# Another order of all pieces in a chunked attention with a gated convolution: the third weight unit behind the second block's keys and queries

## The chip, the cores and the metric

The kernel runs on one core of one Trainium2 chip. The metric is the device time of one execution in microseconds. Engines are named as in the profile: PE (TensorE: matmuls; PEld is its loading of weights), DVE (VectorE), ACT (ScalarE), POOL (GpSimd), and SP (SyncE), which issues all transfers between memory and the chip. PSUM is where matmuls leave their results, here in four banks of two halves each.

## What is computed

Attention runs inside chunks of 64 tokens, for 8 sequences of 576 tokens and 8 heads of 64; its output x is gated by a causal convolution over five tokens and goes through two 512 by 512 matrices, all in float32.

```python
scores = scale * np.matmul(q_c, k_c.transpose(0, 1, 2, 4, 3))      # q_c, k_c, v_c: chunks of 64 tokens
scores = scores - np.max(scores, axis=-1, keepdims=True)
attn = np.exp(scores)
attn = attn / (np.sum(attn, axis=-1, keepdims=True) + 1e-09)
out = np.matmul(attn, v_c)
...
for k in range(K):                                                  # K = 5 taps, per channel
    gate_pre += conv_w[k][None, None, :] * xp[:, k:k + S, :]
gate = 1.0 / (1.0 + np.exp(-gate_pre))
val = x @ w_val
return (gate * val @ w_out).astype(np.float32)
```

## The kernel before

The 4608 tokens are nine groups g of 512, the 512 channels two pairs p of two heads' couples. The work is cut into small functions, called pieces, and one long text, ORDER (lines 19 to 84), lists all 1034 pieces with their arguments. The last loop of the kernel walks through the list and records each piece's instructions, and every engine runs its own share in that order. So ORDER is the whole schedule: on each engine an instruction waits for those that stand before it, and for the data that it needs. SLOTS (lines 87 to 98) says which buffer each piece takes that asks for one (z for buffers of 4 KB a partition, b for PSUM banks, e for the two buffers of exponentials); a buffer that is given out again makes its new writer wait for its old readers.

The pieces that the text speaks of, with g the group, p the pair, c a unit of weights:

- loads on SP: lq, lk, lv (queries, keys, values of g and p; for group 0 the first two also in halves of 256 KB), lw (a unit of w_val "v" or w_out "o", 512 KB), lc (the taps); st and s1 store results.
- weights: each 64-bit number is cut into a high and a low part of fewer bits, so that three cheap products give a float32 product. w1 to w8 make the high part (v_hi, o_hi) on DVE, ACT and POOL, wa and wb the low part (v_lo, o_lo); for units v 1 to v 3 the low part is summed on PE by Q and cast by wc on ACT.
- attention: S multiplies queries by keys (32 small matmuls per g and p, each of which PE runs as two), mx and ng take and scale the maximum on DVE; either sb, ex and sm (subtract, exponential, sum), or ea (16 small exponentials on ACT that sum as they go, 8 for a half) and rc or ra and rr; nm scales on POOL or DVE; T transposes on PE, ec copies to the chip's memory on ACT; A multiplies by the values. xr, xc, xd take its result as high part, as itself and as low part.
- gate: k0 is the first tap on ACT (k0D on DVE), k the other four on DVE (kx and kk do two groups at once), sg the sigmoid on ACT.
- products: V makes one third of the value product (one matmul of 512 columns for group 0, else three), vc copies it on ACT, gs multiplies by the gate on DVE, gr and gd cut the result into high and low part (gd on POOL, gdD on DVE), P is the output product (three matmuls), oc copies it (ocD on DVE). Group 8 ends in smaller pieces, o1 and s1.
- W runs idle matmuls on a zeroed tile before the first data are there: so many of 512 columns, so many of 64.

Every instruction carries line 139 in the profile, since one helper records it; tiles tell them apart: b is a PSUM bank, z and ys are buffers, e_row the exponentials, warm the idle tile.

```python
for piece in ORDER.split(","):
    name, *args = piece.split()
    args = [int(a) if a.isdigit() else a for a in args]
    if name in on_vector:
        fn, on = on_vector[name]
        fn(*args, **{"copy" if fn in (w6, ec, xc, oc, o1, wc) else "on": on})
    else:
        pieces[name](*args)
```

Of the kernel before, what the change touches and what calls it, by code (L numbers as in the profile page):

```python
# [18 lines left out]
ORDER = """zw,lw v 1,zr 1,zr 0,lc,zi,zs 0,zs 1,lw v 3,lw v 2,w1 v 1,w5 c 0,w1 c 0,w2 v 1,w3 v 1,w5 v 1,w4 v 1,w2 c 0,w3 c 0,w5 v 3,  # L19
w7 v 1,w1 v 3,w6 v 1,w8D v 1,w2 v 3,w4 c 0,w3 v 3,W 9 22,Q v 1,lk 0 1 0,lq 0 1 0,w1 v 2,w4 v 3,w2 v 2,w3 v 2,w5 v 2,w6D v 3,  # L20
S 0 1 0,lk 0 0 0,lk 0 1 1,lq 0 1 1,lq 0 0 0,lk 0 0 1,lq 0 0 1,w4 v 2,wc v 1,mx 0 1 0,w6 v 2,w7 c 0,ng 0 1 0,w7 v 2,ea 0 1 0,ra 0 1 0,
W 3,S 0 1 1,w8D v 2,S 0 0 0,mx 0 1 1,w8D c 0,w9,ng 0 1 1,w7 v 3,S 0 0 1,lw v 0,lk 1 0,lq 1 0,lv 0 1,lw o 3,ea 0 1 1,ra 0 1 1,
rr 0 1 0,Q v 2,w8 v 3,mx 0 0,nm 0 1 0,sb 0 0,Q v 3,w5 v 0,w1 v 0,ex 0 0,T 0 1 0,w3 v 0,rr 0 1 1,S 1 0 0,wc v 2,sm 0 0,
nm 0 1 1,S 1 0 1,ec 0 1 0,w2 v 0,A 0 1 0,lk 1 1,lq 1 1,lv 0 0,lv 1 0,wc v 3,mx 1 0,T 0 1 1,nm 0 0,xr 0 1 0,ec 0 1 1,
V 0 2 2 0,sb 1 0,V 0 3 2 1,w5 o 3,A 0 1 1,xc 0 1 0,xr 0 1 1,w4 v 0,T 0 0,xc 0 1 1,xd 0 1 0,V 0 2 3 0,w6D v 0,V 0 3 3 0,
ec 0 0,V 0 2 3 1,w1 o 3,S 1 1 0,w7 v 0,ex 1 0,xd 0 1 1,A 0 0,w8 v 0,k0 0 2,sm 1 0,S 1 1 1,wa v 0,xc 0 0,V 0 0 2 0,V 0 2 2 1,
V 0 0 3 1,V 0 0 2 1,xr 0 0,mx 1 1,V 0 1 2 0,nm 1 0,V 0 0 3 2,V 0 3 3 1,k0 0 0,V 0 3 2 2,V 0 2 3 2,xd 0 0,V 0 3 1 0,
V 0 1 2 1,V 0 0 0 0,V 0 3 3 2,V 0 3 0 0,lw o 0,lw o 2,lw o 1,w5 o 0,k0 0 3,ng 1 1,k 0 0 1,T 1 0,k0 0 1,wbD v 0,V 0 0 0 2,
w2 o 3,V 0 3 2 0,k 0 0 2,V 0 2 1 1,ec 1 0,V 0 2 0 0,V 0 0 1 0,k 0 3 1,V 0 1 0 0,V 0 2 0 1,ea 1 1,V 0 2 0 2,w3 o 3,V 0 2 1 2,
k 0 1 1,V 0 3 1 1,V 0 0 2 2,V 0 1 1 1,w4 o 3,V 0 3 0 1,V 0 2 2 2,V 0 3 1 2,w1 o 1,A 1 0,k 0 0 3,w7 o 3,w1 o 0,V 0 1 3 2,  # L30
# [636 lines left out]
```

## Time and profile before

| | us |
|---|---|
| median of 3 runs | 280.74 (280.64 to 281.19) |
| profiled execution | 281.55 |
| its span, first to last instruction | 279.6 |
| PE busy | 268.9 (96%) |
| DVE busy | 239.5 (86%) |
| ACT busy | 198.7 (71%) |
| POOL busy | 59.4 (21%) |

The profiled execution is a run of its own, 0.8 us above the median; what lies outside the span (some 2 us) is start and end of the program. Times within the trace count from the span's start. Busy shares are averages; what sets the end is read from the chain that ended last, which goes back from the last instruction, at each step to what released it. A piece of that chain called "issue" is time in which an engine waited for nothing that the profile shows.

### The profile page before, as it was taken

Reading aid. Unit: us, or ns where it says so; the run is one execution under the profiler, and the core shown is the slowest. Engines: PE = TensorE matmul, PEld = TensorE weight load, DVE = VectorE, ACT = ScalarE, POOL = GpSimd, SP = SyncE. Lnnn points to the kernel's source line nnn. Section 1 sums busy time; section 2 is a strip of 40 time slices with the busy share of each in tenths; the row PEclk is TensorE's granted clock in tenths of the full one; section 3 lists DMA queues with packets and bytes.
Section 4 is the critical chain, followed back from the end, with each engine's and each line's share of the span. In section 5 each row is a group of like instructions: output and inputs, shape, how many; then the busy total and the mean of one; then the engine's idle time right before and its main releaser. Section 6 shows DMA issues by size and latency. Waiting matters only on the chain.

```text
span 279.6 us, 7851 instructions
## 1 busy us (share of the span) xinstructions
PE 268.9 (96%) x3370; PEld 216.6 (77%) x3370; DVE 239.5 (86%) x303; ACT 198.7 (71%) x368; POOL 59.4 (21%) x58
## 2 busy tenths in 40 slices
PE   6598999999998999999999999999999999999995
PEld 3366778887886888888888888888888888888884
DVE  3979999999999988989898998999999998996020
ACT  5899999999997988895958588837644544614402
POOL 1056242049294003061335001100000000300000
PEclk9999999999999999999999999999999999999999
DMA  6999999763831649540082000000000000050656
GB/s 224 395 409 406 406 407 409 290 225 108 281 149 37 192 150 338 189 131 30 2 292 88 2 5 2 0 0 2 0 0 0 4 0 0 16 212 0 241 209 225
DMA packets 14754, 42.46 MB, mean 152 GB/s; under 512 B 1536, under 2 KB 1792, under 8 KB 14720
## 3 DMA queue, kind: packets, MB, share of 16 engines
q1 hardware_dynamic: 14720, 41.97, 40.7%
q8 instruction: 26, 0.43, 0.6%
q14 instruction: 8, 0.07, 0.1%
HBM read 32.53 MB, written 9.44 MB: 150 GB/s over the span
## 4 chain that ended last, share of the span: by engine, by line
PE 89%; DMA 8%; issue 1%; SPq 0%; ACT 0%
PE b L139 89%; DMA z<-in_v 4%; DMA z<-in_moe_w_val 2%; DMA z<-in_q 2%; SPq L139 0%; ACT z L139 0%
## 5 line engine op out<-in xcount | busy, mean ns | idle before, releaser
L139 PE MATMUL b<-z,v_hi 128*128 128x512 f32 x288 | 97.3, 403 | 1.3 <-issue 1.1
L139 PE MATMUL b<-o_hi,z 128*128 128x512 f32 (+1 forms) x296 | 94.5, 391 | 0.0
L139 DVE SCALAR_TENSOR_TENSOR ys<-ys,cw 128x511 f32<-128x511 f32 (+7 forms) x104 | 84.5, 863 | 0.1
L139 ACT COPY z<-b 128x1024 f32<-128x1024 f32 (+2 forms) x53 | 50.3, 970 | 38.3 <-PE b L139 35.5
L139 PEld LDWEIGHTS b<-z,v_hi 128*128 128x128 f32 x288 | 53.8, 188 | 14.5 <-issue 1.7
L139 PEld LDWEIGHTS b<-o_hi,z 128*128 128x128 f32 x296 | 55.1, 188 | 12.6
L139 PE MATMUL b<-o_lo,z 128*128 128x512 f32 (+1 forms) x148 | 57.4, 388 | 0.0
L139 PE MATMUL b<-z,v_lo 128*128 128x512 f32 x144 | 55.9, 394 | 0.0
L139 POOL TENSOR_TENSOR z<-e_row,rs 128x1024 f32<-128x1024 f32 (+1 forms) x15 | 27.0, 1804 | 47.2 <-DVE rs L139 17.0
L139 PEld LDWEIGHTS b<-o_lo,z 128*128 128x128 f32 x148 | 27.8, 188 | 5.9
L139 PEld LDWEIGHTS b<-z,v_lo 128*128 128x128 f32 x144 | 27.1, 188 | 5.4
L139 POOL TENSOR_TENSOR z<-ys,z 128x1024 fp32r<-128x1024 f32 x4 | 10.0, 2527 | 96.9 <-ACT z L139 96.9
L139 ACT ACTIVATE ys<-ys 128x1024 f32<-128x1024 f32 x16 | 16.8, 1059 | 11.0 <-DVE ys L139 10.8
L139 ACT ACTIVATE e_row<-b,mx 128x64 f32<-128x64 f32 x80 | 23.7, 345 | 0.4 <-DVE mx L139 0.4
L139 DVE TENSOR_TENSOR z<-b,z 128x1024 fp32r<-128x1024 f32 (+1 forms) x19 | 22.0, 1161 | 2.3 <-ACT z L139 1.3
L139 ACT CAST z<-ys 128x1024 fp32r<-128x1024 f32 x16 | 16.5, 1048 | 9.0 <-DVE ys L139 9.0
L139 DVE TENSOR_REDUCE mx<-b 128x16 f32<-128x1024 f32 (+1 forms) x19 | 21.6, 1144 | 1.3 <-PE b L139 1.1
L139 PEld LDWEIGHTS b<-z,z 64*64 64x64 f32 x960 | 15.7, 135 | 7.8 <-DMA z<-in_k 2.6
L139 PE MATMUL b<-z,z 64*64 64x64 f32 x960 | 17.6, 221 | 3.7 <-DMA z<-in_q 3.0
L139 ACT CAST z<-b 128x1024 fp32r<-128x1024 f32 (+1 forms) x19 | 18.7, 991 | 2.1 <-PE b L139 2.1
L139 ACT ACTIVATE ys<-ys,cw 128x512 f32<-128x512 f32 (+1 forms) x25 | 19.2, 811 | 0.0
L139 ACT ACTIVATION_READ_ACCUMULATOR e_row<-b,mx 128x1 f32 x80 | 19.0, 238 | 0.0
(74 smaller groups left out, 308.3 us busy)
## 6 DMA issues: line engine op xcount, KB each, us to landing
out<-z SPq DMA_DIRECT2D x16, 512.0 KB, 3.7
z<-in_q SPq DMA_DIRECT2D x10, 512.0 KB, 7.2
z<-in_v SPq DMA_DIRECT2D x9, 512.0 KB, 5.0
ys<-in_v SPq DMA_DIRECT2D x9, 512.0 KB, 10.1
ys<-in_k SPq DMA_DIRECT2D x9, 512.0 KB, 7.3
z<-in_k SPq DMA_DIRECT2D x7, 512.0 KB, 9.4
ys<-in_q SPq DMA_DIRECT2D x6, 512.0 KB, 10.2
z<-in_moe_w_val SPq DMA_DIRECT2D x4, 512.0 KB, 5.4
```

Source lines behind the costliest of these rows:

```text
L139: return tc.keep_in_program_order(fn(*args, **kwargs))
```

## The change

ORDER and SLOTS are replaced; no function changes. Both lists hold 1034 pieces. Apart from their places, these differ: W 16 16 and W 2 for W 9 22 and W 3; w2 of unit v 2 on DVE instead of w6 of v 3; the first tap of groups 6 and 7 for one couple on ACT (kx 6 1) and that of group 8's last couple on DVE (k0D 8 3); some copies of groups 3, 4 and 6, the scaling of groups 5 and 6 and the gd of group 3 change engines one for one; o1 8 3 goes from DVE to ACT; both gd of group 8 go from DVE to POOL. All else is order. The first and the last line of ORDER and one of SLOTS:

```diff
-ORDER = """zw,lw v 1,zr 1,zr 0,lc,zi,zs 0,zs 1,lw v 3,lw v 2,w1 v 1,w5 c 0,w1 c 0,w2 v 1,w3 v 1,w5 v 1,w4 v 1,w2 c 0,w3 c 0,w5 v 3,
...
+ORDER = """zw,lw v 1,zr 1,zi,zs 0,zs 1,lc,lw v 3,lk 0 1 0,zr 0,lq 0 1 0,w1 v 1,w3 c 0,w2 v 1,w3 v 1,w1 c 0,w2 c 0,w4 v 1,w5 v 3,w1 v 3,
...
-    e="0 1 0 0 0 0 1 1 0 0 0 1 0 1 1 0 1 0",
...
+    e="0 1 0 0 0 0 1 1 0 1 1 0 1 0 1 0 1 1",
```

SP's first transfers, before (in_moe_w_val: a unit of w_val; in_k and in_q: halves of group 0's keys and queries):

```order
L139 DMA z_76<-in_moe_w_val 128x1024
L139 DMA raw_cw<-in_moe_conv_w 128x40
L139 DMA z_90<-in_moe_w_val 128x1024
L139 DMA z_92<-in_moe_w_val 128x1024
L139 DMA z_152<-in_k 128x512
L139 DMA z_154<-in_q 128x512
L139 DMA z_181<-in_k 128x512
```

and now:

```order
L139 DMA z_76<-in_moe_w_val 128x1024
L139 DMA raw_cw<-in_moe_conv_w 128x40
L139 DMA z_89<-in_moe_w_val 128x1024
L139 DMA z_91<-in_k 128x512
L139 DMA z_94<-in_q 128x512
L139 DMA z_166<-in_moe_w_val 128x1024
L139 DMA z_91<-in_k 128x512
```

The third unit of weights moved behind the first halves of keys and queries.

ACT around the two first groups of exponentials (e_row<-b,mx, eight each), before; the casts write v_hi from a buffer and v_lo from a PSUM bank:

```order
L139 CAST v_lo<-b_148 128x2x256
L139 CAST v_hi<-z_156 128x2x256
L139 ACTIVATE e_row_65,rs_197<-b_164,mx_191 128x64 x8
L139 ACTIVATE rs_197<-rs_197,e_row_65 128x8
L139 ACTIVATE e_row_65,rs_278<-b_211,mx_246 128x64 x8
L139 ACTIVATE rs_278<-rs_278,e_row_65 128x8
L139 ACTIVATE z_303<-z_268 128x512
```

and now:

```order
L139 ACTIVATE z_186<-z_166 128x512
L139 ACTIVATE e_row_65,rs_193<-b_149,mx_184 128x64 x8
L139 ACTIVATE rs_193<-rs_193,e_row_65 128x8
L139 CAST v_hi<-z_188 128x2x256
L139 CAST v_lo<-b_174 128x2x256
L139 ACTIVATE e_row_65,rs_275<-b_204,mx_231 128x64 x8
L139 ACTIVATE rs_275<-rs_275,e_row_65 128x8
L139 ACTIVATE z_300<-z_221 128x512
```

A cast to v_hi and the cast to v_lo moved from ahead of the first group to between the two.

PE from the transposes of group 0, pair 0 (T, ident with 128x128) to its values (A, x32) and the scores of group 1, pair 1 (S, x16 each), before:

```order
L139 MATMUL b_419<-ident,z_388 128x128 x8
L139 MATMUL b_393<-z_390,v_hi 128x512 x2
L139 MATMUL b_393<-z_390,v_lo 128x512
L139 MATMUL b_439<-z_373,z_375 64x64 x16
L139 MATMUL b_459<-z_434,z_377 64x64 x32
L139 MATMUL b_439<-z_373,z_375 64x64 x16
L139 MATMUL b_515<-z_390,v_hi 128x512
```

and now:

```order
L139 MATMUL b_417<-ident,z_383 128x128 x8
L139 MATMUL b_407<-z_386,v_hi 128x512
L139 MATMUL b_407<-z_386,v_lo 128x512 x2
L139 MATMUL b_407<-z_386,v_hi 128x512
L139 MATMUL b_407<-z_386,v_lo 128x512
L139 MATMUL b_443<-z_432,z_361 64x64 x32
L139 MATMUL b_480<-z_411,z_359 64x64 x32
L139 MATMUL b_519<-z_386,v_hi 128x512
```

Five products of 512 columns stand between transposes and values instead of three, and both halves of the scores follow the values. SP loads these values one place earlier than before, and the keys of group 1, pair 1 behind them.

## Rows read from the trace of the kernel before

**Rows 1.** The page: busy us of each engine with its share of the span and its instructions; from its list of DMA queues the one that brings instructions (packets, MB, share).

```profile
PE 268.9 (96%) x3370; PEld 216.6 (77%) x3370; DVE 239.5 (86%) x303; ACT 198.7 (71%) x368; POOL 59.4 (21%) x58
...
q8 instruction: 26, 0.43, 0.6%
```

**Rows 2.** The chain of work that ended last, in order of time: start, us, what.

```profile
2.10 6.26 DMA z<-in_moe_w_val
...
8.38 5.37 DMA z<-in_q
...
13.77 11.88 DMA z<-in_v
...
25.78 5.95 PE b L139 x118
31.73 0.17 issue
31.90 52.88 PE b L139 x1014
84.78 0.90 issue
85.68 191.00 PE b L139 x1883
```

**Rows 3.** Stretches of 10 us: their mean, then the busy time (and instructions) of PE, PEld, DVE, ACT and POOL, the granted clock of TensorE, the busy share of the DMA engines, and GB/s.

```profile
20.00:30.00 10.00, 9.05 (x220) 7.16 (x209) 9.01 (x14) 9.30 (x16) 6.37 (x4) 1.00 1.03 406
...
50.00:60.00 10.00, 10.00 (x197) 8.36 (x199) 9.78 (x17) 9.97 (x31) 3.17 (x2) 1.00 0.63 241
...
80.00:90.00 10.00, 9.10 (x163) 7.29 (x162) 9.27 (x13) 8.81 (x11) 6.55 (x6) 1.00 0.01 5
```

**Rows 4.** SP's issues in order of time, the thirteenth and the fourteenth: start, duration, what.

```profile
9.03 0.33 SPq L139 DMA_DIRECT2D z<-in_moe_w_val  x1
9.70 0.33 SPq L139 DMA_DIRECT2D z<-in_k  x1
```

**Rows 5.** PE in order of time, with the idle time before a row and what ended it.

```profile
1.19 4.16 PE L139 MATMUL b<-warm 128*128 128x512 bf16 x31 [1.19 <-DVE warm L139]
...
9.82 0.69 PE L139 MATMUL b<-z,z 64*64 64x64 f32 x32 [1.39 <-DMA z<-in_q]
...
18.32 1.16 PE L139 MATMUL b<-z,z 64*64 64x64 f32 x64 [0.43 <-DMA z<-in_q]
...
24.66 0.69 PE L139 MATMUL b<-z,z 64*64 64x64 f32 x32
25.78 1.63 PE L139 MATMUL b<-z,z 64*64 64x64 f32 x96 [0.43 <-DMA z<-in_v]
27.34 0.50 PE L139 MATMUL b<-z,v_hi 128*128 128x512 f32 x1
...
30.69 1.04 PE L139 MATMUL b<-ident,z 128*128 128x128 f32 x8
```

**Rows 6.** ACT in order of time.

```profile
6.44 0.70 ACT L139 ACTIVATE z<-z 128x512 fp32r<-128x512 uint32 x1 [0.33 <-DMA z<-in_moe_w_val]
...
10.08 0.56 ACT L139 CAST v_lo<-b 128x512 fp32r<-128x512 f32 x1
10.82 0.62 ACT L139 CAST v_hi<-z 128x512 fp32r<-128x512 f32 x1 [0.18 <-DVE z L139]
11.69 0.31 ACT L139 ACTIVATE e_row<-b,mx 128x64 f32<-128x64 f32 x1 [0.25 <-DVE mx L139]
...
14.40 0.29 ACT L139 ACTIVATE e_row<-b,mx 128x64 f32<-128x64 f32 x1
...
17.09 0.68 ACT L139 ACTIVATE z<-z 128x512 f32<-128x512 uint32 x1
...
24.05 1.01 ACT L139 COPY z<-b 128x1024 f32<-128x1024 f32 x1 [0.32 <-issue]
...
25.91 0.71 ACT L139 ACTIVATE ys<-ys,cw 128x512 f32<-128x512 f32 x1
```

**Rows 7.** PE in order of time, from 81.7 to 85.7 us.

```profile
81.70 0.40 PE L139 MATMUL b<-o_hi,z 128*128 128x512 f32 x1
82.03 1.16 PE L139 MATMUL b<-ys 64*64 64x64 f32 x64
83.01 1.11 PE L139 MATMUL b<-z,ys 64*64 64x64 f32 x64
84.06 0.50 PE L139 MATMUL b<-z,v_hi 128*128 128x512 f32 x1
84.39 0.39 PE L139 MATMUL b<-z,v_lo 128*128 128x512 f32 x1
85.68 0.50 PE L139 MATMUL b<-z,v_hi 128*128 128x512 f32 x1 [0.90 <-issue]
```

**Rows 8.** Groups of like instructions (all of the trace): how often, busy us and mean ns of one, then idle time before them.

```profile
L139 DVE TENSOR_SCALAR z<-z 128x512 uint32<-128x512 uint32 x16 | 6.7, 417 | 0.0
...
L139 DVE SCALAR_TENSOR_TENSOR z<-z 128x512 uint32<-128x512 uint32 x8 | 5.5, 685 | 0.3 <-ACT z L139 0.3
...
L139 DVE TENSOR_SCALAR mx<-mx 128x8 f32<-128x8 f32 x2 | 0.3, 168 | 0.0
...
L139 DVE COPY z<-b 128x1024 f32<-128x1024 f32 x3 | 3.7, 1220 | 12.2 <-PE b L139 12.2
...
L139 DVE TENSOR_SCALAR ys<-ys,cw 128x1024 f32<-128x1024 f32 x1 | 0.7, 746 | 0.0
...
L139 DVE TENSOR_SCALAR z<-tails,cw 128x512 f32<-128x512 f32 x1 | 0.5, 479 | 0.0
...
L139 DVE TENSOR_TENSOR z<-z,z 128x1024 fp32r<-128x1024 f32 x2 | 2.4, 1222 | 1.1 <-ACT z L139 1.1
...
L139 ACT ACTIVATE z<-z 128x1024 f32<-128x1024 f32 x2 | 2.0, 1054 | 5.6 <-DVE z L139 5.6
...
L139 POOL TENSOR_TENSOR z<-ys,z 128x1024 fp32r<-128x1024 f32 x4 | 10.0, 2527 | 96.9 <-ACT z L139 96.9
```

**Rows 9.** PE in the output products of the last group: three matmuls each.

```profile
267.17 0.63 PE L139 MATMUL b<-o_hi,z 128*128 128x512 f32 x2
...
267.87 0.63 PE L139 MATMUL b<-o_hi,z 128*128 128x512 f32 x2
```

More of the change, by code (lines that the diff above doesn't have):

```diff
@@ new lines @@
+w7 v 1,w2 v 3,w3 v 3,w5 v 1,w4 v 3,w6 v 1,w8D v 1,W 16 16,S 0 1 0,lw v 2,lk 0 1 1,lq 0 1 1,w5 c 0,w6 v 3,w7 v 3,Q v 1,
+lq 0 0 0,lk 0 0 0,lk 0 0 1,lq 0 0 1,mx 0 1 0,w5 v 2,w1 v 2,w4 c 0,ng 0 1 0,w3 v 2,ea 0 1 0,ra 0 1 0,w2D v 2,S 0 1 1,lw v 0,
+lq 1 0,lk 1 0,lv 0 1,w7 c 0,w4 v 2,mx 0 1 1,W 2,S 0 0 0,w7 v 2,ng 0 1 1,w6 v 2,rr 0 1 0,wc v 1,w8D v 2,S 0 0 1,ea 0 1 1,
+ra 0 1 1,nm 0 1 0,Q v 2,mx 0 0,w8 v 3,sb 0 0,T 0 1 0,w5 v 0,Q v 3,lw o 3,w1 v 0,ex 0 0,rr 0 1 1,w8D c 0,w3 v 0,wc v 2,
+S 1 0 0,nm 0 1 1,sm 0 0,w2 v 0,S 1 0 1,ec 0 1 0,T 0 1 1,lq 1 1,lv 0 0,wc v 3,mx 1 0,A 0 1 0,nm 0 0,ec 0 1 1,xr 0 1 0,
@@ new lines @@
+A 0 1 1,sb 1 0,xc 0 1 0,V 0 2 2 0,xr 0 1 1,V 0 3 2 0,lk 1 1,V 0 3 2 1,xc 0 1 1,w1 o 3,T 0 0,w9,w4 v 0,k0 0 2,V 0 3 3 0,
+w3 o 3,V 0 2 3 1,ec 0 0,w7 v 0,V 0 2 2 1,V 0 2 3 0,w6D v 0,V 0 3 3 1,w8 v 0,xd 0 1 0,ex 1 0,A 0 0,xd 0 1 1,w5 o 3,hc 0 1,
+S 1 1 0,sm 1 0,wa v 0,xr 0 0,S 1 1 1,V 0 0 2 0,xc 0 0,V 0 1 2 1,mx 1 1,V 0 1 1 0,nm 1 0,V 0 2 1 0,V 0 1 0 0,w2 o 3,
+V 0 3 0 0,V 0 0 0 0,xd 0 0,k0 0 3,V 0 3 1 0,V 0 0 3 2,V 0 3 0 1,k0 0 0,V 0 2 1 1,V 0 1 3 0,k 0 3 1,T 1 0,wbD v 0,V 0 0 2 2,
+V 0 3 1 2,ng 1 1,k 0 0 1,V 0 0 1 0,lw o 1,lv 1 0,V 0 2 1 2,V 0 3 2 2,k 0 3 2,V 0 2 2 2,V 0 3 1 1,V 0 3 0 2,V 0 0 1 1,
@@ new lines @@
+sb 8 1,k0 5 0,V 4 2 3,k0 4 1,V 5 0 0,hc 5 1,kk 4 2 2,hc 4 0,ex 8 1,hc 4 1,T 7 1,k0 5 1,kk 4 2 3,V 4 2 1,ec 7 1,V 5 0 3,
+k 5 1 1,vc 4 1,A 7 0,sm 8 1,A 6 1,xr 7 0,nmD 8 1,T 8 0,xc 7 0,V 5 1 1,kk 4 2 4,ec 8 0,V 5 0 1,xc 6 1,k 5 0 1,V 5 1 0,xd 7 0,
+V 5 0 2,xr 6 1,V 5 2 0,kk 4 3 2,V 5 1 3,T 8 1,xd 6 1,V 5 3 3,ec 8 1,k 4 0 3,V 5 1 2,kk 4 3 3,A 6 0,vc 5 0,k 4 1 1,A 8 0,
+xr 6 0,A 8 1,xr 8 0,xcD 6 0,V 5 3 1,xc 8 0,xd 6 0,hc 6 0,V 5 2 1,kx 6 0,V 5 2 2,xd 8 0,xr 8 1,V 5 3 2,k 5 0 2,V 6 2 0,
+k 4 0 4,V 5 2 3,kk 4 3 4,V 8 0 0,V 6 3 3,k 5 1 2,sg 5 1,V 5 3 0,xd 8 1,V 6 3 0,vc 5 1,V 6 2 2,kk 6 0 1,sg 4 1,V 8 1 2,
@@ new lines @@
+V 7 3 0,gs 5 0,V 7 2 1,V 7 1 2,gdD 4 0,V 7 2 3,vc 7 0,V 8 3 0,k 3 3 2,vc 6 0,V 8 2 3,kk 6 1 4,k0 8 0,P 4 0 0,kk 6 3 3,
+gr 5 0,P 4 1 2,P 4 0 1,sg 7 0,k 3 3 3,V 8 3 3,kk 6 2 2,vc 7 1,P 4 1 1,sg 6 0,P 4 2 0,kk 6 3 4,V 8 2 1,gdD 5 0,P 4 2 1,
+P 4 0 2,gdD 5 1,V 8 3 1,P 4 2 3,kk 6 2 3,P 4 3 0,gs 6 0,V 8 2 2,P 4 3 2,vc 8 1,gs 7 0,P 5 0 0,gr 6 0,P 4 0 3,k 3 2 3,
+P 5 2 0,kk 6 2 4,P 5 0 3,k 3 1 2,sg 6 1,P 5 2 1,k 3 2 4,P 4 1 0,k 3 0 2,P 5 0 1,gs 6 1,P 4 1 3,P 5 0 2,gdD 6 0,oc 4 0,
+P 4 2 2,sg 7 1,k 3 3 4,P 4 3 1,k0D 8 2,gr 7 0,P 5 2 3,k 8 2 1,P 4 3 3,gs 7 1,P 6 2 0,oc 4 1,P 5 1 1,gr 6 1,st 4 1,P 6 0 0,
@@ new lines @@
+P 3 1 3,gs 8 0,P 3 3 2,P 3 1 2,gs 8 1,gr 8 0,P 3 0 1,gr 8 1,P 6 2 1,P 6 2 3,oc 7 1,gd 8 1,P 3 2 2,ocD 6 1,st 7 1,P 3 1 0,
+P 3 0 2,st 6 1,P 3 1 1,gd 8 0,P 3 0 3,P 3 3 1,ocD 3 0,P 3 3 3,P 3 2 1,st 3 0,st 7 0,P 3 2 3,st 5 1,P 8 3 0,st 6 0,P 8 2 0,
+P 3 3 0,P 8 0 0 0,oc 3 1,P 8 3 2,P 8 3 3,st 3 1,st 5 0,P 8 0 1 0,P 8 0 3 0,st 4 0,P 8 2 3,P 8 3 1,P 8 1 0,P 8 1 2,P 8 2 2,
+P 8 2 1,P 8 1 3,o1 8 2,o1 8 3,P 8 1 1,s1 8 2,s1 8 3,P 8 0 0 1,o1 8 1,P 8 0 2 0,P 8 0 3 1,s1 8 1,o1 8 0 0,P 8 0 1 1,s1 8 0 0,
+P 8 0 2 1,o1 8 0 1,s1 8 0 1"""
```

111 lines of the change are left out of this document (43 added, 68 removed), and 12 rows, old and new, of the table z.

## The prediction

> **What bounds the kernel now.** I read the page's busy times first: TensorE is busy for 96% of the span, VectorE for 86% [rows 1]. The chain that ended last then says where the other 4% lie: three landings of loads up to 25.64 us, and from 25.78 to 276.68 us nothing but matmuls, with two short pieces called "issue", 0.17 us at 31.73 and 0.90 us at 84.78 [rows 2]. So the end is fixed by the time at which TensorE comes to run without gaps, by the matmul work that is left then, and by these two holes. VectorE, ScalarE and GpSimd count only where they make TensorE wait. The reader is to see that there are about 30 us in which an order can gain, and that elsewhere it can only lose.
>
> What the two holes are can be told from counts. TensorE runs 3370 matmuls and 3370 weight loads, and the instruction queue q8 brings 26 packets, 259 instructions each [rows 1]. Between the two holes lie 1014 matmuls [rows 2], with their loads 2028 instructions, or 7.8 packets; with the semaphore instructions that no row counts, about eight. I take both for waits for the next packet of TensorE's own code. Before the second hole, two runs of 64 small matmuls and two large ones, 260 instructions, pass in 2.75 us (82.03 to 84.78), and work goes on 3.65 us after they began [rows 7]; the DMA engines are nearly idle there (share 0.01) [rows 3]. Before the first hole the last 128 matmuls begin about 25.2 us, and work goes on 6.7 us later, at a DMA share of 1.03 [rows 2, 3, 5]. TensorE stood until 25.78 us for a load inside that stretch, so perhaps only 6.1 us of it belong to the code.
>
> **The change, part by part.** The profiled execution took 281.55 us at a span of 279.6, the median of the runs shown is 280.74; I work out differences on the trace and add them to the median. The reordering adds or removes no matmul except idle ones that keep the array running (34 as before).
>
> *Loads.* From the ninth on, SP issues a transfer when the eighth before it has landed; the chain shows it for the twelfth, which follows the landing of the third weight unit at 8.36 us, and by the next two issues the first keys and queries landed about 9.0 and 9.7 us [rows 2, 4]. At 406 GB/s [rows 3] 512 KB take 1.29 us. With keys and queries ahead of the third weight unit, the first scores can start about 8.4 us instead of 9.82 [rows 5]; the unit lands about 9.7, and behind it each place in the queue keeps its time. The longer idle run (16 wide matmuls) ends about 8.9 us if each takes 0.43 us as the first ones do (nine and 22 short ones end at 5.35 [rows 5]); if it does, up to 0.5 us of the 1.4 are lost.
>
> *VectorE and ScalarE up to the second exponentials.* The first maximum waits now for VectorE: behind the landing of the second weight unit (6.4 us [rows 6]) stand four instructions of 0.42 and two of 0.69 us, 3.1 us, so it starts about 9.4, ends at 10.1, and with one word split and two short ones (0.42 and 0.17 each) [rows 8] the first exponentials start at 10.6 to 11.0 instead of 11.69 [rows 6]. They take 2.7 us to the next group (11.69 to 14.40). But the order puts the cast of the third unit and the v_lo eviction, 0.62 and 0.56 us long, between the two groups of exponentials, where they stood ahead of both [rows 6]. So the second group starts at 14.3 to 14.9, against 14.40. I take no change: **the early scores are spent on ScalarE before they reach TensorE.**
>
> *TensorE from 18 to 32 us.* Keys and queries of the second group keep their place, so the score run at 18.32 stays. ScalarE's list from 17.09 to the copy at 24.05 has the same pieces; one weight scaling moves out, one tap of about 0.7 us moves in [rows 6]. That copy feeds the run that waited at 25.78 for values landing at 25.64; these are now one place earlier in the queue, 24.4 [rows 2]. So this run starts when the copy ends, 24.7 to 25.1 us, 0.7 to 1.1 earlier. Ahead of it the order has eight large matmuls instead of five, behind it the two score runs together (96 records took 1.56 us, so 128 take 2.1), and then the cast of its result, which is free only behind the copy, the exponential and a weight scaling, about 27.1 to 27.6. Twelve matmuls at 0.233 later the transposes start at 30.0 to 30.5 instead of 30.69, with one large matmul more done: 0.4 to 0.9 us gained by the data. [...] I take 31.45 and the one matmul: **-0.55 us** (from -0.9 to +0.3).
>
> *The middle.* A change between small and large matmuls costs about 0.1 us: from 81.70 the step to the small run is 0.33 us, and from 84.06 that to the second large matmul is 0.33 too, where 0.23 is usual [rows 7]. From here the orders have 61 and 58 such changes, some of them free: **+0.1**. Scores of group 5 and the values product behind them stand together as before, so the hole of 0.90 stays. The dense stretch near 55 to 60 us meets one load more in the queue; where before the DMA share falls to 0.63 [rows 3], a packet of code can come late there: 0 to 0.9 us, I take **+0.15**. Up to its last tap VectorE has one tap (0.75 us) and one eviction (1.22, which stands behind that tap now) less and one tap (0.48) more [rows 8]; it does not bound TensorE, whose chain has no VectorE piece [rows 2].
>
> *The end.* Group 8's last two subtractions go from VectorE (1.22 us each) to GpSimd (2.53 each) [rows 8]. From the last tap to the end of both it takes a sigmoid (1.05, the first of the two runs beside the last tap), two gate products (2.4), a cast (1.05) and 5.1 us on GpSimd, about 9.6 us, with the hand-overs 10.3. In the order 17 output pieces of 0.70 us (three matmuls, 267.17 to 267.87 [rows 9]) cover that, 11.9 us, where 13 stood: nothing, unless the last tap comes over 1.6 us later than its place. The last copy and store are the same.
>
> Sum: -0.55 + 0.1 + 0.15 = -0.3, so **280.4 us**.
>
> **Rivals.** *Code is no limit (faster).* If the transposes are held by data alone and the hole at 31.73 is gone, the start gives 0.9; if the one at 84.78 shrinks as well, another 0.9. Against it: two idle times without a releaser, eight packets apart. This gives 279.0 to 279.9. [...]
>
> *Code is late in the loaded stretch (slower).* The place is the dense run of scores and values near 57 us, where more loads are outstanding: 260 instructions pass in about 4.5 us, and if the packet needs 6.1 us as at 31.9, TensorE stands 1.0 to 1.5 us. It decides from a wait over about 5 us. With the start anywhere from the forecast's -0.55 to 0 this gives 281.2 to 282.2.
>
> *The early load does not come early (slower, and the change not doing what it says).* Transfers share the engines; if the first queries land less than about 0.6 us earlier, the two pieces between the exponentials cost ScalarE 0.5 us and more, and everything behind follows: +0.2 to +0.8, 281.0 to 281.5.
>
> **How the numbers follow.** Forecast (280.0 to 281.0) 0.52; no limit by code (279.0 to 279.9) 0.25; late code (281.2 to 282.2) 0.13; no early load 0.10. The range from 279.3 to 281.6 leaves out about a fifth. About 0.2% (0.56 us) is what a measurement of this kernel can tell from no change. Faster than 280.18 holds the second case and a quarter of the first, 0.38; slower than 281.30 holds most of the late code and part of the last, 0.15; the rest, 0.47, is within.
>
> **What would show it.** The first scores at about 8.4 to 8.9 us; the second group of exponentials near 14.4; the values run at 24.7 to 25.1; an "issue" hole right behind the transposes near 31 us and one of about 0.9 near 84 us; no other wait of TensorE over 0.3 us. I am wrong if the second group of exponentials starts before 13.8, if the hole near 31 us is missing, if a new one stands between 50 and 65 us, or if TensorE waits for GpSimd after 255 us.

## Result and profile after the change

The changed kernel is slower: 282.29 us (median of 20 runs, 280.44 to 284.32) against 280.72 (20 runs, 279.68 to 282.26), a ratio of 1.0053 with a 95% interval of 1.0032 to 1.0074, or 1.5 us. The profiled execution took 283.19 us at a span of 281.1, 1.6 us above that of the kernel before (281.55); they lie 0.9 and 0.8 us above their medians.

The chain of waits of the changed kernel (start, us, what) answers to [rows 2]:

```profile
1.65 6.08 DMA z<-in_moe_w_val
...
21.52 0.64 PE b L139 x4
...
23.52 8.85 PE b L139 x163
32.38 0.25 issue
32.63 52.83 PE b L139 x1014
85.46 0.65 issue
86.11 33.20 PE b L139 x268
...
119.33 1.02 ACT z L139
...
120.37 4.83 DMA out<-z
...
125.55 1.02 ACT z L139
...
126.60 1.24 DVE z L139
...
127.88 150.22 PE b L139 x1402
```

As many matmuls are left at 32.63 us as at 31.90 before, and at 86.11 as at 85.68. So the start loses 0.73 us; between the two holes nothing is lost (52.83 against 52.88); the second hole is 0.25 shorter; and from it to the end TensorE takes 191.99 us instead of 191.00, of which 0.54 is idle time in a wait that the kernel before did not have. Together 1.42 us, the whole difference of the last matmul's end (278.10 against 276.68). Among PE's idle times by releaser, 0.5 us behind VectorE's z are new.

The start, in the timeline of PE, DVE and ACT (start, duration, what, idle time before it and what ended it); it answers to [rows 5, 6]:

```profile
9.19 0.69 PE L139 MATMUL b<-z,z 64*64 64x64 f32 x32 [1.03 <-DMA z<-in_q]
16.30 0.79 PE L139 MATMUL b<-v_hi,signed 128*128 128x512 f32 x1
26.52 0.69 PE L139 MATMUL b<-z,z 64*64 64x64 f32 x32
7.75 1.10 DVE L139 TENSOR_SCALAR z<-z 128x512 f32<-128x512 f32 x3 [1.82 <-DMA z<-in_moe_w_val]
10.53 0.68 DVE L139 TENSOR_REDUCE mx<-b 128x8 f32<-128x512 f32 x1
11.81 0.32 ACT L139 ACTIVATE e_row<-b,mx 128x64 f32<-128x64 f32 x1 [0.60 <-DVE mx L139]
14.60 0.60 ACT L139 CAST v_hi<-z 128x512 fp32r<-128x512 f32 x1
15.11 0.58 ACT L139 CAST v_lo<-b 128x512 fp32r<-128x512 f32 x1
15.58 0.32 ACT L139 ACTIVATE e_row<-b,mx 128x64 f32<-128x64 f32 x1
```

The second weight unit lands at 7.7 us (VectorE takes it up at 7.75 after 1.82 us of idling) instead of 6.3, and the first queries, which stand behind it in the queue, at 9.05 (TensorE takes them up at 9.19). So the first maximum is hardly earlier than before, and the two ScalarE pieces between the groups of exponentials put the second group at 15.58 instead of 14.40 [rows 6].

The new wait, in the timeline of ACT, DVE and PE:

```profile
125.55 1.01 ACT L139 CAST z<-b 128x1024 fp32r<-128x1024 f32 x1 [1.38 <-DMA out<-z]
126.60 1.23 DVE L139 TENSOR_TENSOR z<-b,z 128x1024 fp32r<-128x1024 f32 x1 [1.03 <-ACT z L139]
127.88 1.09 PE L139 MATMUL b<-ident,z 128*128 128x128 f32 x8 [0.54 <-DVE z L139]
```

A copy (xr 4 1) is written into the buffer from which output block (1, 0) is being stored. The store was issued at 120.37 and took 4.83 us behind the transfers in flight (DMA share 0.97, 0.92 and 0.98 from 120 to 126 us, in steps of 2); the copy waits for it, the difference behind the copy (xd 4 1) waits too, and the transposes T 5 1 wait for the PSUM bank that both read. This comes from the table of buffers (SLOTS), which was replaced with the order.

### The profile page after: what moved, and what is told of

Same layout as the page of the kernel before. It is cut to its first block, busy times and chain, and to the rows that moved or that the text cites. A ratio compares the mean times of both kernels' runs of the same rounds, so it can differ in the third digit from the quotient of the medians.

```text
span 281.1 us, 7859 instructions
## 1 busy us (share of the span) xinstructions
PE 271.6 (97%) x3370; PEld 217.1 (77%) x3370; DVE 236.5 (84%) x300; ACT 199.6 (71%) x369; POOL 67.3 (24%) x60
## 4 chain that ended last, share of the span: by engine, by line
PE 88%; ACT 5%; DMA 4%; DVE 1%; issue 1%; SPq 0%; ACTq 0%
PE b L139 88%; DMA z<-in_moe_w_val 2%; ACT z L139 2%; ACT e_row L139 2%; DMA out<-z 2%; DVE z L139 1%; ACT v_lo L139 0%; SPq L139 0%; DVE mx L139 0%; ACT v_hi L139 0%; ACT rs L139 0%; ACTq L139 0%; DVE cw_h L139 0%
## 5 line engine op out<-in xcount | busy, mean ns | idle before, releaser
L139 DVE SCALAR_TENSOR_TENSOR ys<-ys,cw 128x509 f32<-128x509 f32 (+7 forms) x104 | 84.6, 864 | 0.1
L139 POOL TENSOR_TENSOR z<-e_row,rs 128x1024 f32<-128x1024 f32 (+1 forms) x15 | 27.7, 1848 | 54.9 <-DVE rs L139 25.7
L139 POOL TENSOR_TENSOR z<-ys,z 128x1024 fp32r<-128x1024 f32 x4 | 10.6, 2644 | 88.1 <-ACT z L139 59.0
L139 DVE TENSOR_TENSOR ys<-z,ys 128x1024 f32<-128x1024 f32 x16 | 19.5, 1222 | 3.3 <-ACT ys L139 3.2
L139 ACT COPY ys<-b 128x1024 f32<-128x1024 f32 (+1 forms) x16 | 15.6, 977 | 8.5 <-PE b L139 8.5
L139 ACT ACTIVATE ys<-ys,cw 128x512 f32<-128x512 f32 (+1 forms) x26 | 20.8, 837 | 0.1
L139 PE MATMUL b<-ident,z 128*128 128x128 f32 x136 | 18.2, 274 | 1.5 <-ACT z L139 0.7
```

The lines of the kernel that those rows point to most:

```text
L139: return tc.keep_in_program_order(fn(*args, **kwargs))
```

## Experiments

Ratios are to the kernel before, timed beside it on the same chip. In the edits a line of pieces stands for the place in ORDER; all slots not named keep their buffers.

**One part alone, and undone.** e1 does only the named move in the kernel before, e2 undoes it in the changed one.

```diff
-lw v 3,lw v 2,w1 v 1 ... lk 0 1 0,lq 0 1 0,w1 v 2
+lw v 3,w1 v 1 ... lk 0 1 0,lq 0 1 0,lw v 2,w1 v 2
```

```diff
-lw v 3,lk 0 1 0,zr 0,lq 0 1 0 ... S 0 1 0,lw v 2
+lw v 3,lw v 2,lk 0 1 0,zr 0,lq 0 1 0 ... S 0 1 0
```

> The kernel before with one edit: the load of the third weight unit stands behind the first keys and queries in SyncE's queue, everything else as before. Theory (transfers in flight share the engines, so what the keys gain the second weight unit loses): the weight work on VectorE, which in the kernel before starts at 6.44 us on the second unit's landing, starts 0.5 to 1.3 us later; the first scores come earlier than 9.82 us, at 8.6 to 9.4; the first exponentials do not come before 11.69 but at 11.8 to 12.8; the hole behind the transposes moves from 31.90 to 32.2 to 32.9; time +0.3 to +0.9 us against the kernel before. Rival (the early load is harmless, the loss lies in ScalarE's order): first exponentials at 11.0 to 11.7, hole at 31.5 to 31.9, time -0.4 to +0.1.

> The changed kernel with one edit: the load of the third weight unit stands again ahead of the first keys and queries. Theory (the loss of 0.73 us at 32 us has two legs, the late second unit and the two ScalarE pieces between the exponentials, and the second leg alone keeps it): the second unit lands at 6.3 to 6.6 instead of 7.72 us, the first scores at 9.6 to 9.9, the first exponentials at 11.4 to 11.8 as in both kernels, the second group still near 15.3 to 15.7, the hole at 32.3 to 32.7, time -0.3 to +0.2 us against the changed kernel (282.0 to 282.5). Rival (the load order alone costs it): second group at 14.3 to 14.7, hole at 31.8 to 32.0, time 281.4 to 281.7.

Measured: e1 1.0060 (1.0042 to 1.0078), first exponentials at 13.41 us, hole ending at 33.16. The third unit now landed at 10.1 us, and VectorE and ScalarE work on it ahead of the first maximum. e2 1.0071 (1.0052 to 1.0089): the second unit landed at 7.78, not at 6.4, and the second group came at 16.45. TensorE stood 1.56 us for ScalarE's v_hi in e1 and 3.52 us for the first queries in e2, and then the granted clock was lower for a while (0.50 in 10 to 12 us in e1, in 12 to 14 us in e2). e1 went further in the direction of my theory than it said; e2 missed both. The named move alone costs the kernel before as much as the whole change does, and without it the changed kernel is no faster, so the loss is not that move's alone. What it does to the landing cannot be read from one execution of each (see Landings).

**ScalarE's order.** e3 moves the two pieces behind the second group, and the matmuls that need them behind T 0 1 0.

```diff
-w6 v 2,rr 0 1 0,wc v 1,w8D v 2,S 0 0 1,ea 0 1 1,ra 0 1 1,nm 0 1 0,Q v 2,mx 0 0,w8 v 3,sb 0 0,T 0 1 0
+rr 0 1 0,w8D v 2,S 0 0 1,ea 0 1 1,ra 0 1 1,w6 v 2,wc v 1,nm 0 1 0,mx 0 0,w8 v 3,sb 0 0,T 0 1 0,Q v 2
```

> The changed kernel with the cast of the third weight unit and the first v_lo eviction moved on ScalarE behind the second group of exponentials (and the matmuls that need that cast behind the first transposes on TensorE). Theory: the second group starts at 14.5 to 14.7 instead of 15.68 us, the wait of 0.73 us at 21.5 goes or shrinks to under 0.2, the hole that stood at 32.63 comes at 31.5 to 32.0, time -0.5 to -1.0 us against the changed kernel. Rival (the place of the hole follows the code packet, whatever ScalarE does): hole within 0.2 of 32.63, time within 0.3 of the changed kernel.

Measured 1.0161 (1.0142 to 1.0180). The second group did come at 13.13, 6.88 us behind the second unit's landing (6.25, early in this execution), but the time is 4.5 us above the kernel before. PE, and windows of 2 us (busy us of PE, PEld, DVE, ACT, POOL, granted clock, DMA share, GB/s):

```profile
14.97 0.77 PE L135 MATMUL b<-ident,z 128*128 128x128 f32 x4 [0.95 <-POOL z L135]
16.96 2.08 PE L135 MATMUL b<-z,ident 128*128 128x512 f32 x2 [1.22 <-ACT v_lo L135]
18.05 1.42 PE L135 MATMUL b<-v_hi,signed 128*128 128x512 f32 x1
```

```profile
16.00:18.00 2.00, 1.04 (x2) 0.53 (x3) 0.56 (x1) 2.00 (x4) 0.14 (x1) 0.50 1.03 410
18.00:20.00 2.00, 2.00 (x5) 1.29 (x4) 0.93 (x5) 0.49 (x2) 0.25 (x1) 0.50 1.00 399
20.00:22.00 2.00, 2.00 (x4) 0.70 (x3) 1.39 (x2) 1.04 (x2) 0.89 (x1) 0.50 1.05 418
```

TensorE waited 0.95 and 1.22 us, and from 16 to 22 us its granted clock was 0.50: the row at 18.05 takes 1.42 us, the same matmul in the changed kernel at a granted clock of 1.00 (16.30 above) 0.79. What ScalarE gained is lost in these waits and on the clock; TensorE's order was changed as well, so the waits cannot be put down to ScalarE alone. That the two pieces cost the second group about 1.0 us is shown (6.88 us behind the landing instead of 7.85, the table under Landings), that moving them pays is not.

**The store's buffer.** e4 exchanges the buffers of xr 4 1 and xd 4 1 in the table; e12 repeats it beside the changed kernel (e13).

```diff
-xr 4 1: z5,  xd 4 1: z15
+xr 4 1: z15, xd 4 1: z5
```

> The changed kernel with two buffers exchanged: the float32r copy of group 4's second half (xr 4 1), which took the buffer whose store was issued at 120.37 and landed at 125.19 us, takes that of the difference behind it (xd 4 1), and the other way round. Theory: ScalarE's wait of 1.38 us ahead of 125.55 goes, the wait of 0.54 us of TensorE at 127.88 goes, and nothing fills it: time -0.4 to -0.7 us against the changed kernel. Rival (the hole only moves on, to VectorE's difference, which waits for the same store): a wait of 0.3 to 0.8 us within 4 us of that place, time within 0.2 of the changed kernel.

> The kernel of e4_store_buffer once more, beside the changed kernel on the same chip. Theory (the wait for the store and what follows it are over half of the loss): 0.6 to 1.1 us below the changed kernel of the same call, no wait for the store near 125 us. Rival (the wait is worth only the hole seen at 127.88): 0.3 to 0.6 us below. Second rival (what it gave was the chip): less than 0.3.

> The changed kernel, timed in the same call as e12_store_buffer_again. Both theories: 1.3 to 1.8 us above the kernel before. The second weight unit lands at 6.2 to 7.9 us and the second group of exponentials starts 7.8 to 7.9 us behind it, whichever theory of the landing holds; a landing under 7.0 in this one and in the others with this start speaks for the single execution, over 7.1 in all for the order.

Measured: e4 1.0022 (1.0004 to 1.0041), e12 1.0031 (1.0008 to 1.0053), e13 1.0094 (1.0058 to 1.0129). In e4 neither ScalarE nor TensorE waits there, and nothing fills the gap:

```profile
124.12 1.00 ACT L135 CAST z<-b 128x1024 fp32r<-128x1024 f32 x1
127.21 1.03 PE L135 MATMUL b<-ident,z 128*128 128x128 f32 x8
```

The exchange gives 0.3% by the first comparison and 0.6% by the second, 0.9 to 1.8 us with wide intervals; in the second, where both were timed on one chip, the intervals do not overlap. With the buffers as they were, ScalarE waited for the store in all six executions traced: 1.52 (e3), 1.38 (the changed kernel), 1.03 (e9), 0.62 (e2), 0.53 (h1), 0.39 us (e13); with the exchange in none. TensorE's own wait was 0.70, 0.54 and 0.22 in the first three and none in the others: it begins where the store is more than about 0.8 us late. So the loss varies with one landing, between nothing and about 0.9 us here (the idle time is 0.2 short of it, as the next rows show), and the median difference is at the upper end of that or beyond it.

e13, the changed kernel once more, shows what is lost when the store lands early enough for TensorE. The transposes T 5 1 and the matmul ahead of them, in the changed kernel's profile and in e13's, and then the end of e13's chain:

```profile
126.94 0.39 PE L139 MATMUL b<-o_hi,z 128*128 128x512 f32 x1
127.88 1.09 PE L139 MATMUL b<-ident,z 128*128 128x128 f32 x8 [0.54 <-DVE z L139]
```

```profile
125.91 0.39 PE L139 MATMUL b<-o_hi,z 128*128 128x512 f32 x1
126.15 1.03 PE L139 MATMUL b<-ident,z 128*128 128x128 f32 x8
```

```profile
32.02 0.35 issue
32.38 243.88 PE b L139 x2897
```

From start to start the two rows are 0.94 us apart with the wait and 0.24 without it: it cost 0.70 us, not 0.54, since one matmul begins before the one ahead of it has ended. And e13 runs all 2897 matmuls behind the first hole in 243.88 us, the 52.88 and 191.00 of the kernel before [rows 2] without its hole. So in this execution the new order loses nothing behind the first hole. It is no typical one: its time, 281.26 us, is the lowest of seven with a median of 282.96.

**Landings.** e9 and e10 are both kernels unchanged, once more.

> The changed kernel once more, unchanged, for a second set of landings. Theory one (how late the second weight unit lands is a matter of the single execution): anywhere from 6.2 to 7.9 us, and whatever it is, the second group of exponentials starts 7.8 to 7.9 us behind it. Theory two (the new load order makes it late): 7.1 to 7.9 us again. The wait near 127 us hangs on how fast one store lands (4.8 us in the execution seen): 0 to 0.8 us.

> The kernel before once more, unchanged. Theory one: the second unit lands anywhere from 6.2 to 7.9 us. Theory two (its load order keeps it early): 6.2 to 6.8 as in the three executions with this start. The hole near 85 us hangs on how fast a packet of code comes: 0 to 0.9 us.

They took 282.29 and 281.73 us. Beside every execution with an untouched start (us, from the trace; e15 has ten idle matmuls more):

| start | second unit lands | second exponentials | values run A 0 0 |
|---|---|---|---|
| new (h2) | 6.44 | 14.29 | 25.76 |
| new (e9) | 7.02 | 14.87 | 25.83 |
| new (e5) | 7.12 | 14.97 | 25.91 |
| new (e12) | 7.26 | 15.11 | 26.04 |
| new (e13) | 7.39 | 15.24 | 26.17 |
| new (after) | 7.72 | 15.58 | 26.52 |
| new (e4) | 7.84 | 15.68 | 26.61 |
| old (before) | 6.33 | 14.40 | 25.78 |
| old (e6) | 6.68 | 14.17 | 25.48 |
| old (h1) | 6.71 | 14.28 | 25.59 |
| old (e10) | 7.28 | 14.76 | 25.69 |
| old (e15) | 7.61 | 15.10 | 25.82 |

The landing varies with the execution: either order has early and late ones. That the new order makes it later on average is not excluded (the middle rows are 7.26 and 6.71). What differs is what follows. In the new start the second group stands 7.85 us behind the landing in all seven rows and the values run 18.8 behind it in six. In the old one the second group follows too (7.5 us behind in four rows of five), but the values run stays within 25.5 to 25.8, whatever lands. The middle rows of the values run, 26.04 and 25.69, put the loss of the start at 0.35 us; the 0.74 between the first two profiles is near the upper end.

**Hybrids.** h1 is the old order up to T 1 0 and the new one behind it, h2 the reverse.

```diff
-ORDER(before)
+ORDER(before up to T 1 0), then what is left of ORDER(after)
```

> Hybrid: the order of the kernel before up to the transposes of group 1's first half (T 1 0, about 31 us), from there the order of the changed kernel. Theory of two parts: the changed order loses about half in its first 32 us and half behind them (0.54 us of it where a copy waits for a store), so this hybrid is +0.5 to +1.0 us against the kernel before, with the first hole at 31.5 to 32.2 and a wait of 0.3 to 0.7 near 127 us. Rival one (the start is the whole loss): -0.2 to +0.2. Rival two (the start costs nothing, what the profile showed there was one execution's late landing): +1.2 to +1.8.

> The other hybrid: the changed order up to T 1 0, from there the order of the kernel before. Theory of two parts: +0.4 to +0.9 us against the kernel before, first hole at 32.2 to 32.9, the hole of 0.9 near 85 us as in the kernel before, no wait near 127. Rival one (the start is the whole loss): +1.2 to +1.8. Rival two (the start costs nothing): -0.3 to +0.2.

Measured 1.0069 (1.0043 to 1.0094) and 1.0112 (1.0085 to 1.0140): 1.9 and 3.1 us. The first lies just above its second rival, and its interval reaches into it; the second is more than any of its cases allowed. The seam brings waits of its own (h1: 0.22 us for GpSimd at 41.13; h2: 1.39 us for a load of keys at 46.11), so the sums tell nothing of the halves. h2's start does: with the unit at 6.4 us it ran up to the second exponentials nearly as I had forecast it (DVE, then ACT).

```profile
6.46 1.10 DVE L135 TENSOR_SCALAR z<-z 128x512 f32<-128x512 f32 x3 [0.59 <-DMA z<-in_moe_w_val]
10.52 0.31 ACT L135 ACTIVATE e_row<-b,mx 128x64 f32<-128x64 f32 x1 [0.28 <-PE b L135]
14.29 0.31 ACT L135 ACTIVATE e_row<-b,mx 128x64 f32<-128x64 f32 x1
```

**Thinning out the small matmuls.** e5 (on e4) and e6 (on the kernel before) put large matmuls between S 5 1 1 and A 3 1.

```diff
-S 5 1 1,A 3 1,k0 1 2,nm 4 0,sm 4 1,P 0 2 1,xr 3 1,mx 5 1,V 3 0 0,nm 4 1
+S 5 1 1,k0 1 2,nm 4 0,sm 4 1,P 0 2 1,mx 5 1,V 3 0 0,A 3 1,xr 3 1,nm 4 1
```

```diff
-A 3 1,nm 4 0,k0 3 0,sm 4 1,V 3 0 0,xr 3 1,P 0 3 3,mx 5 1
+nm 4 0,k0 3 0,sm 4 1,V 3 0 0,P 0 3 3,A 3 1,xr 3 1,mx 5 1
```

> The changed kernel with the two buffers exchanged as in e4_store_buffer, and with the values product A 3 1 (64 small matmuls), which stood right behind the 64 small ones of S 5 1 0 and S 5 1 1, moved behind two groups of large matmuls (P 0 2 1, V 3 0 0). Theory (the hole of 0.65 us at 86.11 is a wait for TensorE's own code, since 256 instructions pass there in under 3 us): the hole shrinks to under 0.3, time 0.3 to 0.6 us below e4_store_buffer. Rival (the hole hangs on something else, and only moves): a hole of 0.5 to 0.9 us between 83 and 88 us, time within 0.2 of e4_store_buffer.

> The kernel before with A 3 1 moved behind V 3 0 0 and P 0 3 3 in the same way, nothing else. Theory (wait for code): the hole of 0.90 us at 85.68 shrinks to under 0.4, time -0.4 to -0.9 us against the kernel before, which beats both kernels. Rival: a hole of 0.6 to 1.0 us remains between 83 and 88 us, time within 0.2 of the kernel before. Second rival (group 3's copies, now 1.4 us later, make a later large matmul wait): hole gone, but a wait of 0.3 us or more for ScalarE or VectorE between 86 and 95 us.

Measured: e5 1.0063 (1.0038 to 1.0089), e6 1.0019 (1.0005 to 1.0032). No hole stands there in either, but the wait of e6's second rival comes (the values product, and ScalarE's copies of it, are 1.4 us later): 0.12 us in e6, and 0.94 in e5, more than the hole of 0.56 in e4. For the new order the missing hole shows nothing, since e8, e12 and e13 lack it without any thinning; in the old order all six executions with this stretch and its count as they were (before, e1, e7, e10, e14, h2) have one of 0.42 to 0.97 us, so there e6 speaks for the theory. PE of e5:

```profile
84.86 1.16 PE L135 MATMUL b<-z,z 64*64 64x64 f32 x64
85.95 0.50 PE L135 MATMUL b<-o_hi,z 128*128 128x512 f32 x1
89.95 0.50 PE L135 MATMUL b<-z,v_hi 128*128 128x512 f32 x1 [0.94 <-ACT z L135]
```

**Code borders.** e11 (on e4) puts 28 matmuls more ahead of everything, e15 ten more in the kernel before. The holes without a releaser stand multiples of 256 of TensorE's records apart, give or take two (counted below); every such place, with a hole or without, I call a border.

```diff
-W 16 16
+W 12 48
```

```diff
-W 9 22
+W 9 32
```

> The kernel of e4_store_buffer with the idle run at the start cut differently: 12 wide and 48 short matmuls instead of 16 and 16, about as long, so that 28 matmuls and 28 weight loads more stand ahead of all else. Theory (the holes without a releaser are waits for the next block of TensorE's code): they stay at the same instruction counts, so the first comes 28 matmuls earlier in the program, ahead of the transposes T 1 0 instead of in them, and the second inside the small matmuls of A 3 1 instead of two large ones behind them; each 0 to 1 us. Rival (they belong to the work: the transposes, the first large product): holes, where there are any, at T 1 0 and behind P 0 2 1 as in the changed kernel. Time within 0.4 us of e4_store_buffer by both.

> The kernel before with ten more short idle matmuls at the start (32 instead of 22), where TensorE waits for its first loads anyway: 20 instructions more stand ahead of all else, and each border between blocks of 256 comes ten matmuls earlier in the program. Theory (the holes without a releaser stand where a block of code is used up faster than the next one comes): the border that stood at 85.7 us, right behind 128 small matmuls, now falls among them, with fewer of them in its block, and the hole of 0.6 to 1.0 us seen there in four executions of this start shrinks to under 0.3; the first hole stays under 0.4; time -0.3 to -0.9 us against the kernel before. Rival (the holes belong to the work around them): hole of 0.6 to 1.0 us at 85 to 86 us as before, time within 0.25.

Measured: e11 1.0361 (1.0324 to 1.0398), 290.62 us; e15 1.0057 (1.0037 to 1.0077). PE of e11, and windows of it:

```profile
26.51 1.97 PE L135 MATMUL b<-z,z 64*64 64x64 f32 x119
31.03 0.41 PE L135 MATMUL b<-z,z 64*64 64x64 f32 x9 [2.55 <-issue]
65.34 1.03 PE L135 MATMUL b<-z,ys 64*64 64x64 f32 x57
69.03 0.49 PE L135 MATMUL b<-z,ys 64*64 64x64 f32 x7 [2.66 <-issue]
```

```profile
28.00:30.00 2.00, 0.48 (x35) 0.35 (x24) 0.93 (x2) 2.00 (x3) 0.49 (x1) 1.00 1.03 406
30.00:32.00 2.00, 0.97 (x11) 0.76 (x11) 0.51 (x1) 2.00 (x4) 0.41 (x1) 0.80 1.01 406
32.00:34.00 2.00, 2.00 (x6) 1.61 (x5) 2.00 (x3) 0.72 (x2) 1.50 (x1) 0.50 1.04 414
```

In the midst of 128 small matmuls, nine and seven before their end, TensorE stands 2.55 and 2.66 us without a releaser; then its granted clock is lower for a while (0.50 in 32 to 34 and in 70 to 72 us). And PE of e15:

```profile
31.12 0.64 PE L135 MATMUL b<-z,v_hi 128*128 128x512 f32 x2 [0.68 <-issue]
85.40 0.34 PE L135 MATMUL b<-z,ys 64*64 64x64 f32 x8 [0.39 <-issue]
```

The second hole moved into A 3 1 and shrank (0.90 to 0.39), the first grew (0.17 to 0.68). Counted in the trace, the holes of over 0.1 us from 18 us on stand behind 448, 705, 960 to 962, 1984, 2241, 3008 to 3010 and 4545 records of TensorE (matmuls, weight loads and the 58 to 64 semaphore instructions among them) in all kernels here: each 192 to 194 more than a multiple of 256. The place follows the count and not the work, as theory had it; that moving it pays, as I expected of e15, was wrong. The packets of the queue that brings instructions (26 of 16 KB each in the changed kernel's profile) show what TensorE waits for there: each of the 39 holes ends 1.2 to 1.6 us after such a packet has ended (in the changed kernel 31.16 and 32.63 us, 84.54 and 86.11; in e11 29.58 and 31.03, 67.63 and 69.03). That packet began 0.2 to 1.2 us after the border before was passed in the holes at 85 to 88 us, and 3.2 to 4.4 us after it in those at 31 to 35 us, where the DMA share is about 1 (1.01 to 1.04 in e11's rows above). Which borders show differs between executions of one program, and most show in none: the changed kernel had holes at 32.63 and 86.11 us in its first profile, at 84.86 and 139.69 in e9, at 32.38 alone in e13.

**Earlier requests.** e7 (on the kernel before) and e8 (on e4) put the small load lc behind the second unit's, e14 also moves the short steps on it back; e16 is e14 with W 9 32.

```diff
-lc,zi,zs 0,zs 1,lw v 3,lw v 2,w1 v 1,w5 c 0,w1 c 0,w2 v 1,w3 v 1
+zi,zs 0,zs 1,lw v 3,lc,lw v 2,w1 v 1,w2 v 1,w3 v 1,w5 c 0,w1 c 0
```

```diff
-lc,lw v 3,lk 0 1 0,zr 0,lq 0 1 0,w1 v 1,w3 c 0,w2 v 1,w3 v 1
+lw v 3,lc,lk 0 1 0,zr 0,lq 0 1 0,w1 v 1,w2 v 1,w3 v 1,w3 c 0
```

```diff
-w1 v 1,w2 v 1,w3 v 1,w5 c 0,w1 c 0 ... w2 c 0,w3 c 0 ... w3 v 3 ... w4 c 0
+w1 v 1,w2 v 1,w3 v 1 ... w3 v 3,w5 c 0,w1 c 0,w2 c 0,w3 c 0 ... w3 v 2,w4 c 0
```

> The kernel before with the small load of the convolution weights (lc) behind that of the second weight unit in SyncE's queue, so that the unit and all that follows it is asked for 0.45 us earlier, and the two short weight steps on it one or two places later on VectorE and ScalarE. Theory (TensorE's first 32 us follow the landings of the first loads nearly one to one): first queries land 0.3 to 0.5 us earlier than 9.54 to 9.69, second group of exponentials at 13.7 to 14.1, time -0.2 to -0.5 us against the kernel before. Rival (the transfers share the engines, which are at work from 2 us on, so an earlier request lands no earlier): landings within 0.15 us, time within 0.2.

> The changed kernel with the buffers exchanged as in e4_store_buffer and the small load behind the second weight unit's in the same way. Theory: second unit lands at 6.0 to 7.4 us, the second group of exponentials 7.85 us behind it as in the four executions seen so far, time 0.2 to 0.5 us below e4_store_buffer. Rival (no earlier landing): time within 0.2 of e4_store_buffer.

> The kernel before with the small load of the convolution weights behind the second weight unit's, as in e7_old_small_load_later, where it then landed at 6.54 us and VectorE stood 1.79 us for it ahead of the weight work. Here the short steps on it (w1 c, w2 c, w3 c, w4 c, w5 c 0) stand behind that work. Theory (the landings set the start): the second unit lands at 5.5 to 6.5, first exponentials at 10.8 to 11.4 instead of 11.69, the second group at 13.5 to 14.1 instead of 14.40, time -0.4 to -0.9 us against the kernel before, which beats both. Rival (the code of TensorE holds the first hole at 31.5 or later, whatever lands): time within 0.25.

> The kernel of e14_old_small_load_last with the ten idle matmuls more. Theory: both gains add, -0.6 to -1.3 us against the kernel before, the fastest of all versions here. Rival (the start gains nothing by earlier landings, or the code holds it): like e15_old_ten_more_idle within 0.25.

Measured: e7 0.9984 (0.9961 to 1.0007), e8 1.0016 (0.9993 to 1.0039), e14 0.9985 (0.9965 to 1.0005), e16 1.0078 (1.0051 to 1.0106). The second unit lands at 5.4 to 5.7 us in all four, so asking earlier helps it. Little of it reaches the end. In e7 the second group comes at 15.18 (the small load, now later, holds VectorE for 1.79 us), and in e14 the first queries land no earlier (9.84) and the granted clock is 0.50 from 12.0 to 15.4 us. In e8 the values run starts at 25.07, 1.54 us before that of e4, but holes of 0.50 and 0.60 us at two borders leave 0.45 of it behind the second of them (32.34 us, in e4 32.79). e7 and e14 are faster than the changed kernel, and than the kernel before by 0.15%, which either interval alone leaves open. In e16 the first hole is 1.33 us: the ten matmuls that help at 85 us cost more at 32.

## Why the prediction was wrong

*Loads: the step that failed first.* I took the second weight unit's landing as fixed (6.4 us, from one execution) and queries at 8.4. It lands anywhere from 6.3 to 7.8, with the new and the old order, and by the table the new start passes that on to the values run undiminished in six rows of seven, while the old one does not. At 6.44 us (h2) the numbers of that step hold within 0.1: first scores at 8.31 (I said 8.4), first exponentials at 10.52 (10.6 to 11.0), the second group at 14.29 (14.3 to 14.9). At 7.72 the exponentials come 1.3 us later. The rival "the early load does not come early" had most of the mechanism (the two pieces on ScalarE, everything behind follows) and a price of 0.2 to 0.8; its condition was about the queries, which came 0.63 us earlier in the profile, just outside it, while it was the weight unit that held the first maximum. That transfers share the engines shows in the changed kernel too: from 20 to 30 us the loads in flight moved 408 GB/s together, at a DMA share of 1.03. The start measured +0.73 where I forecast -0.55.

*TensorE from 18 to 32 us.* The values run at 24.7 to 25.1 was a mis-sized term apart from that: it came at 25.76 even in h2. From 21.52 on TensorE does not wait ahead of it in the changed kernel; it is still busy with what follows the transposes there, which I had not counted. The term of -0.55 has an error of its own: 31.45 against 31.90 and a matmul of 0.233 would make -0.68, and the matmul was no gain, since as many are left behind the hole in both kernels. The 31.45 rests on the time at which a packet of code is asked for, and no run shows that; they show that the packet ahead of this hole ended at 30.42 us before and at 31.16 now, and that the hole ended 1.48 and 1.47 us behind it.

*The holes.* Right in place in the first profile, 0.25 and 0.65 us, though e9 lacks the first and e13 the second. Right in nature too: they end 1.47 and 1.57 us behind packets of instructions, and in e11 and e15 they move with the count of instructions, so "code is no limit" falls. Between the holes at 32.63 and 86.11 lie 2048 records, eight times 256. At most borders no hole shows (at 23 of the 25 from 18 us on in that profile), but behind dense runs of small matmuls 2.55 and 2.66 us do in e11.

*The middle: the step that was missing.* I added up transitions (+0.1) and one late packet (+0.15); from 32 to 85 us nothing was lost (-0.05), and no hole came in the loaded stretch. The 61 and 58 changes of size are 59 and 58 behind the first hole by the traces, with transposes as a size of their own. But I read the new table of buffers for nothing, a term put at zero without a reason. Its reuse of a buffer under a slow store costs 0.54 us of idle time in the profiled execution, and without it (e4, e12) the kernel is 0.9 to 1.8 us faster by the medians. By the medians this is the larger part of the loss; the traces show less than 1 us of it.

*The end.* Right: the last 3 us are as before, and TensorE does not wait for GpSimd.

None of the four cases reached 282.29 us; the late code in the loaded stretch (281.2 to 282.2) came nearest, by a hole that never came.

*What stays open.* From the second hole to the end the first profile loses 0.45 us beside the idle time of the wait. Some 0.2 of it is the wait's own, and in e13 next to nothing is lost there, so it varies with the execution too. The exchange of buffers gives more in the medians than any one trace shows, and no execution near e13's median of 282.96 us was traced there. And since ten idle matmuls alone move this kernel by 1.4 us (e15), some part of any difference between two orders may be where the code borders fall; I have not separated that for the changed order.

## What to carry to other kernels

Take the time of a landing from several executions, or cost both orders by how far each follows it; one trace is one draw. When a change replaces a table of buffers, look in it for every buffer that is still being stored when it is written again. Where TensorE runs many small matmuls, count instructions: holes stood multiples of 256 apart here, one behind a dense run cost 2.66 us (e11), and idle matmuls put ahead moved them (28 in e11, ten in e15).

## What the hardware showed that I had not expected

The same request, made at 1.63 to 1.65 us, lands between 6.26 and 7.84 us in 16 executions. In the changed kernel's trace a few packets are slow: three of 4 KB, begun between 4.3 and 4.5 us, took 1.13, 1.17 and 1.71 us, where 0.159 is usual, and the sixteen parts of the second unit land from 5.21 to 7.72 us (before: from 5.18 to 6.33). Waits of 1 to 3.5 us on TensorE were followed by some 3 to 7 us at a granted clock of 0.50 in e1, e2, e3, e11, e14 and e16, while one of 2.26 us for the first queries in e4 and one of 1.69 us in e15 were followed by none.
